# Start of a fused attention and gated-MLP kernel: x's first tile turned ahead of the modulation columns, K's upper half loaded ahead of x's second tile, the first chunk of x taken tile by tile, and units 0 and 1 by pairs of heads

## The chip, the cores and the metric

One core of a Trainium2 chip runs the whole kernel. TensorE (PE) multiplies matrices and turns tiles, VectorE (DVE), ScalarE (ACT) and GpSimd (POOL) do elementwise work, and SyncE's queue (SP) issues nearly all DMAs. Each engine takes its instructions in the order of the program; they meet only through semaphores. The metric is the device time in microseconds (us) of one execution.

## The reference

The inputs are x (2048 x 512), a cache of keys and values (8 groups of 2048 x 128), wq, wo, the MLP's weights, a conditioning vector c and its matrix w_mod, all bf16.

```python
mod = (_silu(c) @ w_mod).reshape(c.shape[0], 6, 1, -1)
sa, ca, ga, sb, cb, gb = ...
h = _layernorm(x, axis=-1) * (1 + ca) + sa
x = x + ga * _A_ref(h, A_k_cache, A_v_cache, A_wq, A_wo)
h = _layernorm(x, axis=-1) * (1 + cb) + sb
x = x + gb * _B_ref(h, B_w_in, B_w_sp, B_b_sp, B_w_out)
```

`_A_ref` is attention with 32 query heads on 8 key/value groups (4 heads to a group): q = h wq, p = softmax(q kT / sqrt(128)), o = p v, then o wo. `_B_ref` is a gated MLP: z = gelu(h w_in), its second half is normalised and mixed over positions by w_sp, multiplied with the first half, then w_out.

## The kernel before

**Units.** The attention is cut into 128 units. Unit u is one group of keys and values and one tile of 128 rows of x (16 tiles, four of them a *chunk* of 512 rows). An iteration `it` of the main loop (from L1455) has 8 slots. In slot i of iteration u, `qk(u, i)` (L1016) computes scores into one of two `s_ps` buffers in PSUM and ACT writes their exp to `pTs[u]`. A unit from 1 on multiplies, for all four heads, two key tiles a slot: two matmuls of 512 columns (L1068), then one exp (L1075). Unit 0 goes by pairs of heads: its slots 0 to 3 do heads 0 and 1 for all sixteen key tiles, slots 4 to 7 heads 2 and 3, with four matmuls of 256 columns a slot (L1052, L1059). `pv(u, i)` (L1116) is one of eight parts of p v (8 matmuls, L1124); parts 0 to 3 are heads 0 and 1, parts 4 to 7 heads 2 and 3; after each four, DVE takes the reciprocal of the row sums and writes `onorm` (L1135, L1136). In the early units, p v of unit u runs in iteration u + 1. Unit 0, going by pairs, starts in its own slots 4 to 7 and ends in slots 0, 2, 4 and 6 of iteration 1.

**What stands around a slot.** `at(it, slot, fn)` runs `fn` ahead of the slot's scores; `fill[it, slot]` runs behind its `pv`. This order of emission is the order of each engine's instructions.

**The start.** SP's queue loads x's tile 0, w_mod's first two parts (`wmod_a`, the columns for sa and ca, in two loads), half of wq's first group (heads 0 and 1), K's lower half by rows in two loads (`k_nat`), then x's tile 1, wq's second half, x's tiles 2 and 3, K's upper half by a DMA transpose (L759), v, the rest of x, and wo. PE multiplies zeros (`warm`, L777) while it waits, then computes the modulation columns (`mod_first`, L874; one matmul of one column for each of 4 x 8 blocks), turns x's tile 0 (L909) between the third and fourth of `mod_first`, and turns K's lower half (`k_turn`, L864), which DVE copies to `kT0`. `modc` (L916) holds 1 + ca and sa; `ln1_mod` (L804) applies them to turned x and writes `hT`. `first_q(0)` (L935) projects q of tile 0 for heads 0 and 1, and `first_q(1)` for heads 2 and 3.

**The first chunk.** x's tiles 1 to 3 are normalised and turned within the first units: `ln_stats` (L695, DVE), `rstd_of` (L675, POOL), `normalise` (L685, DVE), `ln1_turn` (L814: turns on PE, `ln1_mod` on DVE). Tile 1 is done by itself, tiles 2 and 3 together (one `rstd_of`, one turn of both, L1294), and q by `qproj` (L955; matmuls L967, copy on DVE L978): tile 1 in slots 4 and 5 of unit 0, tiles 2 and 3 together in 256 columns in unit 1. The buffers `misc` and `o_ps` in PSUM have two banks each.

**Later chunks.** `ln1_at` (L1302) sets the same for chunks 1 to 3: statistics, norm, four DMA transposes (`ln1_dma`, L833), and the modulation in place (`ln1_dma_mod`, L838). Chunk 1 has its statistics ahead of slot 7 of unit 0, norms ahead of slot 2 of unit 1, DMAs ahead of slot 3, and modulation ahead of slot 2 of unit 2. Its projection for units 4 to 7 (`set_fill`, b = 1, matmuls of 512 columns) starts in slot 5 of unit 2, two matmuls a slot, and needs the modulated chunk.

Of the kernel before, what the change touches and what calls it, by code (L numbers as in the profile page):

```python
# [15 lines left out]
P = 128  # L16
# [559 lines left out]
def kernel(  # L576
# [173 lines left out]
    nc.sync.dma_start(out=wqs[0][:, :, pairs[0]], in_=wq_dram[:, :, pairs[0]])  # L750
    load_k_nat(0)
    load_k_nat(1)
    nc.sync.dma_start(out=x_sb[:, 1, :], in_=x_dram[:, 1, :])
    nc.sync.dma_start(out=wqs[0][:, :, pairs[1]], in_=wq_dram[:, :, pairs[1]])
    nc.sync.dma_start(out=x_sb[:, 2:CT, :], in_=x_dram[:, 2:CT, :])

    kT0 = early.tile([P, SK], BF16, name="kT")
    groups[0] = dict(kT=kT0)
    nc.sync.dma_start_transpose(out=kT0[:, HK:SK], in_=A_k_cache[0, 0, HK:SK])  # L759
    load_v(0)  # L760
    for ch in range(1, NCH):
        tiles = slice(ch * CT, (ch + 1) * CT)
# [48 lines left out]
            op1=ALU.add,  # L811
        )

    def ln1_turn(j0, n, xns, banks=("misc", "o_ps")):  # L814

        ch, c0 = j0 // CT, (j0 % CT) * P
        hT = hT_of(ch)
        for half in range(2):
            t_ps = bank(banks[half])[:].bitcast(BF16).rearrange("p (k q) -> p k q", k=2)
            for k in range(2):  # L820
                dt = half * 2 + k
                for jj in range(n):
                    nc.tensor.transpose(
                        t_ps[:, k, jj * P : (jj + 1) * P],
                        xns[jj][:, dt * P : (dt + 1) * P],
                        ident[:],
                    )
            for k in range(2):
                dt = half * 2 + k
                dst, src = hT[:, dt, c0 : c0 + n * P], t_ps[:, k, 0 : n * P]  # L830
                ln1_mod(dst, src, dt)

    def ln1_dma(j0, n, xns):  # L833
        hT = hT_of(j0 // CT)
# [64 lines left out]
    nc.vector.tensor_copy(out=sc_bf[:], in_=sc[:])  # L899
    xns0 = ln1_norm(0, 1, rstd0)  # L900
    mc_ps = bank("misc")
    warm(11)
    for kt in range(NDT - 1):
        mod_first(kt, mc_ps)
    warm(1)

    x_ps = bank("misc")[:].bitcast(BF16)[:, 0:D]
    for dt in range(NDT):
        nc.tensor.transpose(  # L909
# [1 line left out]
        )  # L911
    xT0 = res.tile([P, D], BF16, name="xn1", bufs=4)
    nc.vector.tensor_copy(out=xT0[:], in_=x_ps)
    warm(2)
    mod_first(NDT - 1, mc_ps)
    nc.vector.tensor_copy(out=modc[:, 0 : 2 * NDT], in_=mc_ps[:, 0 : 2 * NDT])  # L916
    warm(1)
    k_copy = k_turn((0, 1, 2, 3))
    hT_of(0)
    for dt in range(NDT):  # L920
        dst, src = hTs[0][:, dt, 0:P], xT0[:, dt * P : (dt + 1) * P]
# [7 lines left out]
            )  # L929
        else:  # L930
            ln1_mod(dst, src, dt, nc.gpsimd if dt == 3 else nc.vector)
    k_copy()
    qTs = {0: early.tile([P, REP, 512], BF16, name="qT")}

    def first_q(hf):  # L935
# [14 lines left out]
        )  # L950

    first_q(0)
    k_turn((4, 5, 6, 7))()

    def qproj(b, heads, c0, n, banks=("misc", "misc")):  # L955

# [59 lines left out]
    def qk(u, i):  # L1016
        g, j = divmod(u, NT)
        b, jj = g * NCH + j // CT, j % CT
        if i == 0:
            if homes[u] == "wsp":  # L1020
                pTs[u] = wspp.tile([P, NT, 512], BF16, name="wsp")
            else:
                pTs[u] = late.tile([P, NKT, 512], BF16, name=homes[u], bufs=1)
            if by_rows(u):
                rsums[u] = stat.tile([P, NSLOT], FP32, name="rs")
        s_ps = bank2()
        if by_rows(u):
            hh, half = divmod(i, 2)
            for c in range(2):
                k0 = (2 * half + c) * 512  # L1030
                nc.tensor.matmul(  # L1031
                    s_ps[:, c * 512 : (c + 1) * 512],
                    lhsT=qTs[b][:, hh, jj * P : (jj + 1) * P],
                    rhs=groups[g]["kT"][:, k0 : k0 + 512],
                    start=True,
                    stop=True,
                )
            nc.scalar.activation(  # L1038
                out=rows_of(u, hh)[:, half * HK : (half + 1) * HK],
                in_=s_ps[:],  # L1040
                func=ACT.Exp,
                scale=inv_sqrt_dh,
                accum_out=rsums[u][:, i : i + 1],
            )
            if half == 1:
                at(*divmod(u * NSLOT + i + 1, NSLOT), lambda: turn_rows(u, hh))
            return
        if u == 0:
            pair, k0 = i // 4, i % 4 * 4
            qs = slice(pair * 256, (pair + 1) * 256)  # L1050
            for kt in range(4):
                nc.tensor.matmul(  # L1052
                    s_ps[:, kt * 256 : (kt + 1) * 256].rearrange("p (r q) -> p r q", r=2),
                    lhsT=groups[g]["kT"][:, (k0 + kt) * P : (k0 + kt + 1) * P],
                    rhs=qTs[b][:, 2 * pair : 2 * pair + 2, jj * P : (jj + 1) * P],
                    start=(kt % 2 == 0),
                    stop=(kt % 2 == 1),
                )
            nc.scalar.activation(  # L1059
                out=pTs[u][:, k0 : k0 + 4, qs],  # L1060
                in_=s_ps[:].rearrange("p (k q) -> p k q", k=4),
                func=ACT.Exp,
                scale=inv_sqrt_dh,
            )
            return
        for h in range(2):
            kt = 2 * i + h
            nc.tensor.matmul(  # L1068
                s_ps[:, h * 512 : (h + 1) * 512].rearrange("p (r q) -> p r q", r=REP),
                lhsT=groups[g]["kT"][:, kt * P : (kt + 1) * P],  # L1070
                rhs=qTs[b][:, :, jj * P : (jj + 1) * P],
                start=True,
                stop=True,
            )
        nc.scalar.activation(  # L1075
            out=pTs[u][:, 2 * i : 2 * i + 2, :],
            in_=s_ps[:].rearrange("p (k q) -> p k q", k=2),
            func=ACT.Exp,
            scale=inv_sqrt_dh,
        )  # L1080
# [197 lines left out]
    wsp = [None] * NCH  # L1278

    fill = {}  # L1280
    def first_norm():
        first["r1"] = ln1_stats(1, 1)
        ln_stats(mv1, 2, x_sb[:, 2, :])
        first_q(1)
        first["x1"] = ln1_norm(1, 1, first["r1"])

    def first_turn():
        ln1_turn(1, 1, first["x1"])
        ln_stats(mv1, 3, x_sb[:, 3, :])
        first["r2"] = rstd_of(mv1[:, 2:4, :], 2, "ln1")  # L1290

    fill[0, 1] = [first_norm]
    fill[0, 2] = [first_turn]
    at(0, 5, lambda: first.update(x2=ln1_norm(2, 2, first["r2"])))  # L1294
    at(0, 7, lambda: ln1_turn(2, 2, first["x2"], ("misc", "misc")))
    next_q = qproj(0, list(range(REP)), P, P)
    fill[0, 4], fill[0, 5] = next_q[0:8], next_q[8:16]
    rest_q = qproj(0, [0, 1], 2 * P, 2 * P) + qproj(0, [2, 3], 2 * P, 2 * P)
    for i in range(6):
        fill[1, i + 1] = rest_q[(8 * i + 2) // 3 : (8 * i + 10) // 3]  # L1300

    def ln1_at(ch, stats, norm, turn):  # L1302
        st = {}
# [2 lines left out]
        at(norm[0], norm[1] + 1, lambda: ln1_dma(ch * CT, CT, st["x"]))  # L1306
        at(*turn, lambda: ln1_dma_mod(ch))

    ln1_at(1, (0, 7), (1, 2), (2, 2))
    ln1_at(2, (2, 4), (3, 1), (4, 5))  # L1310
    ln1_at(3, (5, 1), (5, 5), (7, 4))
    at(1, 4, lambda: nc.sync.dma_start(out=wmod_b, in_=wmod_dram[:, :, 2 * D : NMOD]))
# [142 lines left out]
    for it in range(NU + 6):  # L1455
        if it < NU:
            if it % CT == 0 and it // CT + 1 < NB:
                set_fill(it // CT + 1)
        elif it == NU:
            free_a.close()  # L1460
            z2p = fast.enter_context(tc.tile_pool(name="z2p", bufs=1))
            zs["z2"] = z2p.tile([P, NT, FH], BF16, name="z2")
        pvs = [u for u in range(max(it - 5, 0), min(it, NU)) if pv_at(u) == it]
        wos = [u for u in range(max(it - 8, 0), min(it, NU)) if wo_at(u) == it]
        wf = [fn for u in wos for fn in wo_proj(u)]
        for i in range(NSLOT):
            for fn in later.pop((it, i), []):
                fn()
            if it < NU:
                qk(it, i)  # L1470
            if it < 2:
                if it == 0 and i >= NSLOT // 2:
                    pv(0, i - NSLOT // 2)
                elif it == 1 and i % 2 == 0:
                    pv(0, (NSLOT + i) // 2)
            elif len(pvs) == 1:
                pv_part(pvs[0], i, NSLOT)
            elif pvs:
# [196 lines left out]
```

## Time and profile before

| What | Value |
|---|---|
| Time, median of 3 runs | 1307.65 us (1307.35 to 1308.0) |
| The profiled execution's own time | 1308.09 us |
| Its span, first to last instruction | 1306.1 us |
| Granted TensorE clock | 0.999 |
| First score matmul | 9.84 us |
| Unit 1, 2, 3, 4: first score matmul | 18.28, 26.60, 35.08, 44.31 us |
| ACT in unit 1 | 8 exps in 7.66 us |
| HBM | 21.37 MB read, 2.10 MB written |

A profile is one execution. Busy time is the sum of an engine's instructions; a line of the timeline gives start and duration in us, the engine, the kernel's line, the operation, output <- inputs, and in brackets the idle time before it and what released it. A matmul's duration holds its way through the array, so pace is read from one start to the next. "SPq" is a DMA being issued by SP's queue, not its transfer. The change lies within the first 45 us.

### The profile page before, as it was taken

To read this page: it belongs to the slowest core of one execution; us is meant where nothing else is said; L and a number is where in the kernel's file an instruction comes from. 1 tells how busy PE (TensorE), PEld (TensorE's weight loads), DVE (VectorE), ACT (ScalarE), POOL (GpSimd) and SP (SyncE) were. 2 spreads that over 40 slices of the span, in tenths; PEclk is the share of its full clock that TensorE was granted. 3 is DMA by queue.
4 is the path that set the end of the run, shared out by engine and by line. 5 is a ranking of instruction groups with operands and counts; after the bars stand their busy time and mean duration, and the time that the engine had idled before them with its cause. 6 is when DMAs were issued, how large, how long until landed. Compare 5 with 4: busy or idle time off the path is not lost.

```text
span 1306.1 us, 22924 instructions
## 1 busy us (share of the span) xinstructions
PE 1297.3 (99%) x8818; PEld 706.9 (54%) x8818; DVE 674.0 (52%) x1740; ACT 1112.4 (85%) x1651; POOL 57.1 (4%) x93
## 2 busy tenths in 40 slices
PE   9999999999999999999999999999999999999998
PEld 6665555555555555555555555555555566644445
DVE  5534445544554455445544554455455557684443
ACT  7899999999999999999999999999999989650000
POOL 1000000000000000000000000000000135210000
PEclk9999999999999999999999999999999999999999
DMA  7569999999999999999999999999999931264300
GB/s 185 123 128 190 161 192 184 190 167 187 192 187 167 192 166 186 188 176 183 186 188 173 185 189 183 179 185 169 187 183 175 158 91 33 55 137 97 79 20 31
DMA packets 743878, 203.33 MB, mean 156 GB/s; under 512 B 728144, under 2 KB 742096, under 8 KB 743760
## 3 DMA queue, kind: packets, MB, share of 16 engines
q1 hardware_dynamic: 741312, 199.68, 83.3%
q10 hardware_dynamic: 2448, 2.10, 0.5%
q8 instruction: 71, 1.16, 0.4%
q14 instruction: 47, 0.39, 0.1%
HBM read 21.37 MB, written 2.10 MB: 18 GB/s over the span
## 4 chain that ended last, share of the span: by engine, by line
PE 92%; DVE 0%; POOL 0%; issue 0%
PE o_ps L1103 20%; PE s_ps L1031 19%; PE o_ps L1124 13%; PE s_ps L1068 12%; PE misc L1181 8%; PE misc L967 7%; PE misc L1542 7%; PE s_ps L1372 2%; PE s_ps L1411 2%; PE o_ps L1575 1%; PE s_ps L1575 0%; POOL xacc L1197 0%; POOL x_sb L1198 0%; PE o_ps L846 0%; DVE bnst L697 0%; DVE tmp L1587 0%
## 5 line engine op out<-in xcount | busy, mean ns | idle before, releaser
L1031 PE MATMUL s_ps<-kT,qT 128*128 128x512 bf16 x1184 | 352.1, 379 | 0.2 <-ACT pn L1038 0.2
L1038 ACT ACTIVATE win_sb<-s_ps 128x1024 bf16<-128x1024 f32 x298 | 304.7, 1023 | 3.2 <-ACT win_sb L1038 0.5
L1103 PE MATMUL o_ps<-pT,v 128*128 128x512 bf16 x896 | 265.8, 379 | 0.0
L1075 ACT ACTIVATE pT<-s_ps 128x1024 bf16<-128x1024 f32 x248 | 250.7, 1025 | 16.3 <-PE s_ps L1068 4.6
L1068 PE MATMUL s_ps<-qT,kT 128*128 128x512 bf16 x848 | 252.2, 379 | 1.1 <-ACT pT L1075 1.1
L1174 DVE SCALAR_TENSOR_TENSOR xacc<-misc,rall,xacc 128x512 f32<-128x512 f32 x290 | 217.0, 748 | 54.6 <-PE misc L1181 48.4
L1038 ACT ACTIVATE pn<-s_ps 128x1024 bf16<-128x1024 f32 x196 | 200.5, 1023 | 1.2
L1181 PE MATMUL misc<-wo_g,oT 128*128 128x512 bf16 x512 | 194.0, 379 | 0.1
L1103 PEld LDWEIGHTS <-v 128*128 128x128 bf16 x1184 | 115.9, 98 | 139.7
L1075 ACT ACTIVATE wsp<-s_ps 128x1024 bf16<-128x1024 f32 x176 | 179.5, 1023 | 13.2 <-PE s_ps L1068 5.0
L967 PE MATMUL misc<-hT,wq_g 128*128 128x512 bf16 (+2 forms) x528 | 190.0, 371 | 0.0
L1031 PEld LDWEIGHTS <-qT 128*128 128x128 bf16 x1184 | 115.5, 98 | 103.9 <-issue 0.7
L1124 PEld LDWEIGHTS <-pT 128*128 128x128 bf16 x2048 | 136.8, 98 | 58.2
L978 DVE CAST qT<-misc 128x512 bf16<-128x512 f32 x127 | 87.2, 687 | 155.5 <-PE misc L967 155.5
L1124 PE MATMUL o_ps<-v,pT 128*128 128x129 bf16 x2048 | 157.2, 220 | 0.0
L1092 DVE TENSOR_TENSOR tot<-rs 128x1 f32<-128x1 f32 x296 | 45.5, 154 | 163.9 <-ACT win_sb L1038 110.2
L1068 PEld LDWEIGHTS <-kT 128*128 128x128 bf16 x848 | 82.2, 98 | 85.7 <-DVE qT L978 1.5
L1124 PEld LDWEIGHTS <-wsp 128*128 128x128 bf16 x1408 | 94.3, 98 | 41.5
L1124 PE MATMUL o_ps<-v,wsp 128*128 128x129 bf16 x1408 | 108.5, 220 | 0.0
L1542 PE MATMUL misc<-wsp,z 128*128 128x512 bf16 (+2 forms) x560 | 100.5, 336 | 0.0
L1038 ACT ACTIVATE wmod_a<-s_ps 128x1024 bf16<-128x1024 f32 x98 | 100.2, 1023 | 0.0
L1103 PE MATMUL o_ps<-wsp,v 128*128 128x512 bf16 x288 | 85.7, 379 | 0.0
(111 smaller groups left out, 874.0 us busy)
## 6 DMA issues: line engine op xcount, KB each, us to landing
wo_g<-in_A_wo_dram SPq DMA_DIRECT2D x8, 512.0 KB, 4.9
wq_g<-in_A_wq_dram SPq DMA_DIRECT2D x7, 512.0 KB, 4.1
v<-in_A_v_cache_dram SPq DMA_DIRECT2D x7, 512.0 KB, 4.9
wsp<-in_w_mod_dram SPq DMA_DIRECT2D x1, 2048.0 KB, 8.6
out_dram<-yout ACTq DMA_DIRECT2D x16, 128.0 KB, 1.7
pT<-win_sb SPq DMA_TRANSPOSE x113, 4.8
win_sb<-in_B_w_in_dram SPq DMA_DIRECT2D x1, 1792.0 KB, 7.3
x_sb<-in_A_x_dram SPq DMA_DIRECT2D x3, 512.0 KB, 5.6
```

The lines of the kernel that those rows point to most:

```text
L967: nc.tensor.matmul(ps[0][:, o0 : o0 + n], lhsT=wqs[g][:, dt, hh * DH : (hh + 1) * DH], rhs=hTs[ch][:, dt, c0 : c0 + n], start=(dt == 0), s ...
L978: nc.vector.tensor_copy(out=dst, in_=src)
L1031: nc.tensor.matmul(s_ps[:, c * 512 : (c + 1) * 512], lhsT=qTs[b][:, hh, jj * P : (jj + 1) * P], rhs=groups[g]["kT"][:, k0 : k0 + 512], sta ...
L1038: nc.scalar.activation(out=rows_of(u, hh)[:, half * HK : (half + 1) * HK], in_=s_ps[:], func=ACT.Exp, scale=inv_sqrt_dh, accum_out=rsums[u ...
L1068: nc.tensor.matmul(s_ps[:, h * 512 : (h + 1) * 512].rearrange("p (r q) -> p r q", r=REP), lhsT=groups[g]["kT"][:, kt * P : (kt + 1) * P], ...
L1075: nc.scalar.activation(out=pTs[u][:, 2 * i : 2 * i + 2, :], in_=s_ps[:].rearrange("p (k q) -> p k q", k=2), func=ACT.Exp, scale=inv_sqrt_dh,)
L1092: nc.vector.tensor_tensor(out=tot[:], in0=rs[:, 2 * hh : 2 * hh + 1], in1=rs[:, 2 * hh + 1 : 2 * hh + 2], op=ALU.add)
L1103: nc.tensor.matmul(o_pss[u][:], lhsT=groups[g]["v1"][:, kt, 0:DH], rhs=pTs[u][:, kt, :], start=(kt == 0), stop=(kt == NKT - 1),)
L1124: nc.tensor.matmul(o_ps[:, hh % 2, 0 : DH + 1], lhsT=pTs[u][:, kt, hh * P : (hh + 1) * P], rhs=groups[g]["v1"][:, kt, 0 : DH + 1], start=( ...
L1174: nc.vector.scalar_tensor_tensor(out=xa[:], in0=X_ps[:], scalar=scale, in1=xa[:], op0=ALU.mult, op1=ALU.add)
L1181: nc.tensor.matmul(ps[0][:], lhsT=oTs[u][:, hh, :], rhs=groups[g]["wo"][:, hh, :], start=(hh == 0 or each), stop=(hh == REP - 1 or each),)
L1542: nc.tensor.matmul(g_pss[f][:, :n], lhsT=z2[:, st, f * P : (f + 1) * P], rhs=wsp[t][:, st, c0 : c0 + n], start=(st == 0), stop=(st == NT - ...
```

## The change

- The order of SP's queue: K's upper half (the DMA transpose) comes ahead of x's tile 1, wq's second half and x's tiles 2 and 3.
- x's tile 0 is turned ahead of all `mod_first`; the `warm` matmuls are 10 and 3 in place of 11, 1, 2 and 1; both `k_turn` follow `first_q(0)`.
- `first_q(1)` moves from behind slot 1 to behind slot 2 of unit 0, ahead of tile 1's norm.
- Tiles 1, 2 and 3 of x are each normalised, turned (four turns into one bank) and projected alone: `tile_stats`, `tile_norm`, `ln1_turn`, `tile_q`. Tile 3's statistics come behind slot 3 of unit 1, its turn behind slot 7, its q in slots 1 and 3 of unit 2.
- Unit 1 goes by pairs of heads, as unit 0. Its p v starts in its own slots 4 to 7 and ends in slots 0, 2, 4 and 6 of iteration 2; unit 0's ends in slots 0 to 3 of iteration 1.
- Chunk 1's statistics come behind slot 7 of unit 0 and slot 0 of unit 1, its `rstd_of` ahead of slot 1, its norms behind slot 2, its DMAs ahead of slot 3 of unit 1, and its modulation ahead of slot 4 of unit 2.

```diff
     load_k_nat(1)
+    kT0 = early.tile([P, SK], BF16, name="kT")
+    groups[0] = dict(kT=kT0)
+    nc.sync.dma_start_transpose(out=kT0[:, HK:SK], in_=A_k_cache[0, 0, HK:SK])
     nc.sync.dma_start(out=x_sb[:, 1, :], in_=x_dram[:, 1, :])
     nc.sync.dma_start(out=wqs[0][:, :, pairs[1]], in_=wq_dram[:, :, pairs[1]])
     nc.sync.dma_start(out=x_sb[:, 2:CT, :], in_=x_dram[:, 2:CT, :])
-    nc.sync.dma_start_transpose(out=kT0[:, HK:SK], in_=A_k_cache[0, 0, HK:SK])
     load_v(0)
...
-    def ln1_turn(j0, n, xns, banks=("misc", "o_ps")):
...
+    def ln1_turn(j, xn):
+
+        ch, c0 = j // CT, (j % CT) * P
         hT = hT_of(ch)
+        t_ps = bank("misc")[:].bitcast(BF16)[:, 0:D]
+        for dt in range(NDT):
+            cols = slice(dt * P, (dt + 1) * P)
+            nc.tensor.transpose(t_ps[:, cols], xn[:, cols], ident[:])
+        for dt in range(NDT):
+            ln1_mod(hT[:, dt, c0 : c0 + P], t_ps[:, dt * P : (dt + 1) * P], dt)
...
-    warm(11)
-    for kt in range(NDT - 1):
-        mod_first(kt, mc_ps)
-    warm(1)
+    warm(10)
     x_ps = bank("misc")[:].bitcast(BF16)[:, 0:D]
...
-    warm(2)
-    mod_first(NDT - 1, mc_ps)
+    for kt in range(NDT):
+        mod_first(kt, mc_ps)
     nc.vector.tensor_copy(out=modc[:, 0 : 2 * NDT], in_=mc_ps[:, 0 : 2 * NDT])
-    warm(1)
-    k_copy = k_turn((0, 1, 2, 3))
+    warm(3)
...
-    k_copy()
...
     first_q(0)
-    k_turn((4, 5, 6, 7))()
+    for kts in ((0, 1, 2, 3), (4, 5, 6, 7)):
+        k_turn(kts)()
...
-        if u == 0:
+        if u < 2:
             pair, k0 = i // 4, i % 4 * 4
...
+    def tile_stats(j):
+        first[j] = ln1_stats(j, 1)
+
+    def tile_norm(j):
+        xn = res.tile([P, D], BF16, name="xn2", bufs=2)
+        normalise(xn[:], x_sb[:, j, :], mv1[:, j, 0:1], first[j][:, 0:1])
+        first[j] = xn
+
+    def tile_q(j):
+        return qproj(0, list(range(REP)), j * P, P)
+
+    def chunk_stats(j0):
+        for j in range(j0, j0 + 2):
+            ln_stats(mv1, j, x_sb[:, j, :])
+
+    fill[0, 1] = [lambda: tile_stats(1)]
+    fill[0, 2] = [lambda: first_q(1), lambda: tile_norm(1)]
+    fill[0, 3] = [lambda: ln1_turn(1, first[1]), lambda: tile_stats(2)]
+    at(0, 5, lambda: tile_norm(2))
+    q1, q2, q3 = tile_q(1), tile_q(2), tile_q(3)
+    fill[0, 5], fill[0, 6] = q1[0:8], q1[8:16] + [lambda: ln1_turn(2, first[2])]
+    fill[0, 7] = [lambda: chunk_stats(CT)]
+    fill[1, 0] = [lambda: chunk_stats(CT + 2)]
+    at(1, 1, lambda: first.update(r=rstd_of(mv1[:, CT : 2 * CT, :], CT, "ln1")))
+    fill[1, 1] = q2[0:8]
+    fill[1, 2] = q2[8:16] + [lambda: first.update(x=ln1_norm(CT, CT, first["r"]))]
+    at(1, 3, lambda: ln1_dma(CT, CT, first["x"]))
+    fill[1, 3] = [lambda: tile_stats(3)]
+    fill[1, 5] = [lambda: tile_norm(3)]
+    fill[1, 7] = [lambda: ln1_turn(3, first[3])]
+    fill[2, 1], fill[2, 3] = q3[0:8], q3[8:16]
+    at(2, 4, lambda: ln1_dma_mod(1))
...
-    ln1_at(1, (0, 7), (1, 2), (2, 2))
     ln1_at(2, (2, 4), (3, 1), (4, 5))
...
-            if it < 2:
-                if it == 0 and i >= NSLOT // 2:
-                    pv(0, i - NSLOT // 2)
-                elif it == 1 and i % 2 == 0:
-                    pv(0, (NSLOT + i) // 2)
+            if it < 2 and i >= NSLOT // 2:
+                pv(it, i - NSLOT // 2)
+            elif it == 1:
+                pv(0, i + NSLOT // 2)
+            elif it == 2 and i % 2 == 0:
+                pv(1, (NSLOT + i) // 2)
+            elif it < 3:
+                pass
             elif len(pvs) == 1:
```

More of the change, by code (lines that the diff above doesn't have):

```diff
@@ L755 @@
     nc.sync.dma_start(out=x_sb[:, 2:CT, :], in_=x_dram[:, 2:CT, :])
-    kT0 = early.tile([P, SK], BF16, name="kT")
-    groups[0] = dict(kT=kT0)
-    nc.sync.dma_start_transpose(out=kT0[:, HK:SK], in_=A_k_cache[0, 0, HK:SK])
     load_v(0)
@@ L812, in ln1_mod @@
         )
-    def ln1_turn(j0, n, xns, banks=("misc", "o_ps")):
-        ch, c0 = j0 // CT, (j0 % CT) * P
+    def ln1_turn(j, xn):
+        ch, c0 = j // CT, (j % CT) * P
         hT = hT_of(ch)
[L818 to L831, printed above, removed]
+        t_ps = bank("misc")[:].bitcast(BF16)[:, 0:D]
[4 more added lines that the diff above has]
+            ln1_mod(hT[:, dt, c0 : c0 + P], t_ps[:, dt * P : (dt + 1) * P], dt)
     def ln1_dma(j0, n, xns):
@@ L1280 @@
     fill = {}
[L1281 to L1300, printed above, removed]
+    def tile_stats(j):
[26 more added lines that the diff above has]
+    at(2, 4, lambda: ln1_dma_mod(1))
     def ln1_at(ch, stats, norm, turn):
```

## The prediction

> **What bounds the kernel now.** I read the page first (busy time, slices, the chain that ended last), then busy time by stage, the waits, and the timelines of the first 62 us, the only stretch that the change touches.
>
> ```profile
> span 1306.1 us, 22924 instructions
> PE 1297.3 (99%) x8818; PEld 706.9 (54%) x8818; DVE 674.0 (52%) x1740; ACT 1112.4 (85%) x1651; POOL 57.1 (4%) x93
> ...
> PE 92%; DVE 0%; POOL 0%; issue 0%
> ```
>
> TensorE (PE) bounds the kernel as a whole. So the change pays only through PE time without useful work ahead of the point where PE runs unbroken, and costs only through new PE waits. Busy time by stage, cut at the first score matmul and at the starts of units 1, 2, 3 and 4:
>
> ```profile
> core 0: us, PE busy (x) PEld busy (x) DVE busy (x) ACT busy (x) POOL busy (x), PEclk, DMA share, GB/s
> 0.00:9.84 9.84, 8.28 (x68) 4.14 (x69) 4.05 (x16) 2.35 (x4) 2.31 (x12) 1.00 0.87 253
> 9.84:18.28 8.44, 7.81 (x101) 6.93 (x100) 6.53 (x19) 7.00 (x8) 1.75 (x4) 1.00 1.16 302
> 18.28:26.60 8.32, 7.26 (x67) 4.84 (x65) 7.08 (x20) 8.26 (x9) 1.28 (x2) 1.00 0.19 45
> 26.60:35.08 8.48, 8.48 (x87) 5.87 (x88) 3.76 (x11) 7.32 (x9) 0.00 (x0) 1.00 0.66 193
> 35.08:44.31 9.23, 9.23 (x91) 6.16 (x90) 6.04 (x16) 7.47 (x9) 1.27 (x2) 1.00 0.74 166
> ```
>
> Unit 0 is limited now by PE, now by ACT; unit 1 by ACT (8.26 of 8.32), with PE idle about 1.1; from unit 2 on PE has no gap. In unit 1 VectorE (DVE) is at 7.08 of 8.32: hardly slack. The rows that matter below:
>
> ```profile
> 5.89 2.25 SPq L759 DMA_TRANSPOSE kT<-in_A_k_cache_dram  x1
> 8.14 0.17 DVE L916 COPY modc<-misc 128x8 f32<-128x8 f32 x1 [0.19 <-PE misc L874]
> 9.84 1.03 PE L1052 MATMUL s_ps<-qT,kT 128*128 128x256 bf16 x8 [0.24 <-ACT qT L947]
> 23.42 1.38 DVE L686 TENSOR_SCALAR xn<-x_sb,mv,rstd_ln 128x512 bf16<-128x512 bf16 x4 [0.97 <-POOL rstd_ln L682]
> 23.87 6.01 SPq L836 DMA_TRANSPOSE hT<-xn  x4
> 26.60 0.60 PE L1068 MATMUL s_ps<-qT,kT 128*128 128x512 bf16 x2 [1.06 <-ACT pT L1075]
> 31.21 1.38 DVE L805 TENSOR_SCALAR hT<-hT,modc 128x512 bf16<-128x512 bf16 x4 [4.67 <-DMA hT<-xn]
> 32.01 0.59 PE L967 MATMUL misc<-hT,wq_g 128*128 128x512 bf16 x2
> 35.08 0.59 PE L1068 MATMUL s_ps<-qT,kT 128*128 128x512 bf16 x2
> ```
>
> First scores start at 9.84. Unit 2 starts late, at 26.60, where PE had waited for q (copied 25.86 to 26.54). The second chunk of x is normalised at 23.42, turned by four DMAs from 23.87, usable from 31.6 (first modulated slice), and first used at 32.01: 0.4 to spare.
>
> **Paces** (start to start in these timelines): a slot's scores on PE 0.435 (4 of 256 columns or 2 of 512); a PV part 0.455; 8 projections of 128 columns 0.44; 4 turns 0.23; one exp on ACT 0.945, released 0.64 after its scores start (0.71 in the 512 form), freeing its bank 0.14 after its pace. DVE: statistics of a tile 0.80, normalising 0.32 (0.13 more until a reader starts), reciprocal with onorm 0.54, q copy 0.585, modulating a 128-column slice from PSUM 0.26. POOL: 0.17 after the statistics, then 0.31 and 0.58 (one tile) or 1.05 (four), 0.06 to the reader. Followed engine by engine in program order, these paces put the kernel before at 26.54, 35.13 and 37.77 for the starts of unit 2, unit 3 and slot 2 of unit 3; the trace has 26.60, 35.08 and 37.71.
>
> **The start.** K's DMA transpose now takes the place in SP's queue of x's second tile (3.70), and no longer waits for the modulation load (0.7 of SP wait). It holds SP for 2.25, so x's second tile is issued at 5.95 instead of 3.70, wq's second half at 6.4 and x's tiles 2-3 at 6.9. The loads behind (v, the rest of x, wo) come about 0.8 earlier than now, as the 0.7 is gone. On PE, x's tile 0 is normalised at 5.54, so its four turns run at 5.60 to 6.03 (0.107 each, half the pace of the filler matmuls' 0.43). The 33 modulation matmuls need 0.69 + 0.22 (as at 5.92 and 7.76): 6.94. The last modulation slice was issued at 1.6 and took 4.9: it is there at 6.5. Now modc came 0.18 after its last matmul, first_q 0.57 after modc's start: 7.69. Fillers fall from 15 to 13 and lie in the shadow of modc. K's turns follow first_q by 0.51 (as 8.71 to 9.22), their copy starts 0.42 later and lasts 0.42, with 0.05 to the reader: first scores at 9.1, 0.74 earlier. Both ends: 8.7 if the turns run at full pace, 10.15 by the third rival.
>
> **Slots 0 to 3.** Slot 2 waits for the first exp: 9.1 + 0.64 + 1.08 = 10.81. first_q(1), now behind it, runs at 11.25, its DVE copy at 11.95, and behind that copy on DVE the norm of tile 1 at 12.28; its turn on PE waits 0.5 until 12.73. Slot 4 comes at 12.96 (now 13.38). q and turns by tile cost PE nothing: 32 matmuls of 0.055 for 16 of 0.1085; DVE pays 12 slices of 0.26 for what were 4 of 0.26 and 4 of 0.32, 0.8 more.
>
> **Slot 4 to the end of unit 1.** PE is full: 0.89 a slot, 0.44 more in four of them (q of tiles 1 and 2), 0.23 for tile 2's turn: 12.96 + 12 x 0.89 + 4 x 0.44 + 0.23, about 25.65 at the end of unit 1's last PV part. There the new order puts tile 3's turn, and DVE is not there. DVE's queue: tile 2's slices end 18.33; reciprocal and onorm 18.87; the four statistics of the next chunk 22.07; POOL's rstd of it 23.66; four norms 24.94; reciprocal and onorm 25.48; only then tile 3's statistics 26.28; POOL 27.40; norm 27.85. **PE waits 2.2**, and behind the waiting turn stands unit 2's first score, so ACT starves too (its last exp of unit 1 ends near 26.2, the next starts at 28.8). Now tiles 2 and 3 share one rstd and are turned at 16.94, long before. Unit 2 starts at 28.08 against 26.60.
>
> **Units 2 and 3.** Unit 2 has four PV parts less (moved into unit 1) and tile 3's 16 projections more: 0.94 less for PE, so ACT's pace sets it: 28.08 + 7.75 = 35.83, against 8.48 now. The next chunk's turned x is no new wait: its norms start at 23.66 (now 23.42), DMAs and modulation keep 7.8, but the q copy of tile 3 is ahead on DVE: first slice from 32.47, usable 32.9, first needed 33.1. Then DVE is late once more: modulation to 33.76, statistics to 36.96, reciprocal and onorm 37.50, and only then the copy of b=1's head 0 (38.17), whose bank head 2 wants at 38.05: 0.12. Slot 2 of unit 3: 38.60.
>
> **Sum**, after against before: lead at unit 1's start 17.64 - 18.28 = -0.64; unit 1 10.44 - 8.32 = +2.12; unit 2 7.75 - 8.48 = -0.73; first two slots of unit 3 +0.14: +0.89, less the 0.06 by which the paces overshoot: +0.83. Behind it order and work are the same. The profiled execution took 1308.09 (span 1306.1 and 2.0 around it), so 1308.9 for it; against the median of 1307.65: **1308.5**. That is 0.06%, and about 0.2% (2.6 us) is what a measurement of this kernel can tell from no change: no change, on the slow side.
>
> **Rivals.**
>
> *The turn of tile 3 finds its data* (DVE is quicker than its rows, or the wait is absorbed). Against it: four statistics, five norms and two round trips to POOL in one in-order queue. What is late next caps it: q of tile 3 needs slices that are no sooner; and b=1's first projection cannot start before the turned chunk, 31.45 + 0.4 = 31.85 against 32.01, so -0.2: 1307.5. Only if that chain shortens too does ACT's pace rule: unit 3 at 25.9 + 7.6 = 33.5, 1.6 earlier: 1306.0. Even then 0.2% is not reached without a start near 8.1.
>
> *Slower: x's second tile is late.* It is queued behind K's transpose. Until 10.36 its landing is hidden by first_q(1)'s copy; from there each us is a us for turn(1), slot 4 and all DVE work behind. Loads of x landed 2.2 to 8.0 after issue in the first 40 us, so between 8.15 and 13.95: price 0 to 3.6. From 12.2 on the total passes 2.6: 1310.3 and more, at 13.95 1312.1. For it: the DMA engines are full (share 1.09 to 1.33) until 18. Against it: the bytes ahead are 1.6 MB and K's 0.26 MB, and the queue moved 2.3 MB by 9.5. I take 9.6, nearest to K's landing (3.70 + 5.3 = 9.0) and 0.13 MB more. The Trainium skill (DMA: Bandwidth & Descriptors, Queues, rings and completion order) has each DMA engine consume descriptors in ring order; by that rule x follows K's packets and the landing is this 9.4 to 9.6, which no run here has shown yet.
>
> *PE's fast pace comes later.* Fillers run at 0.43 until 5.9, a single one at 6.61 still takes 0.59 (0.38 later), and two at 7.33 show 0.21: the pace doubled near 7. The granted clock reads 1.00 throughout. The new order gives PE one filler less before that and four turns instead. If it doubles some 3 us later (the fillers ran 5.8 at half pace), three fillers end at 8.2, first_q at 9.05, K's copy at 10.1: first scores 10.15, +1.05 on everything: 1309.6. The Trainium skill (TensorE: Matmul & The Clock Gate, Part 1 and Part 4) holds that busy windows of about 3.4 us lift the gate and that transposes do not count as busy in the same way, which speaks against this change; by that rule this rival's time would be the forecast. The trace agrees with a doubling after some 5.8 us of activity and shows nothing of the turns' part in it.
>
> **How the numbers follow.** Forecast 56% (1308.0 to 1309.2 with a start between 8.7 and 9.4). Tile 3 in time 12%, of it 5 beyond 0.2%. x late 20%, 18 of them beyond 12.2. Late fast pace 12%, 4 beyond, where x is late as well. So faster 5%, same 73%, slower 22%. Range 1306.2 to 1311.2: from near the first rival's lower time to a landing of x at 13.1; about 2 in 10 are left out.
>
> **What would show it.** Right: a PE wait of about 2.2 for DVE's xn ahead of tile 3's turn, with ACT idle then; first scores near 9.1; unit 2 shorter than before. Wrong: unit 2 starting before 26.6; no such wait; statistics of tile 1 beginning after 10.4; first scores after 9.8; a wait of b=1's first projection for the turned chunk.

## The result, and the profile after

| | before | after |
|---|---|---|
| Time, median of 22 runs each on one chip | 1307.59 us (1307.28 to 1308.02) | 1309.39 us (1308.95 to 1310.84) |
| The profiled execution's time, its span | 1308.09, 1306.1 us | 1309.50, 1307.0 us |
| First score matmul | 9.84 us | 9.06 us |
| Units 1, 2, 3, 4 | 18.28, 26.60, 35.08, 44.31 us | 17.64, 28.02, 35.63, 45.16 us |

The ratio of after to before is 1.0017, with a 95% interval of 1.0011 to 1.0023: slower, by less than the 0.2% that the text on record took as what can be told from no change, though the interval lies off 1. The 22 times of after are in two groups, 12 from 1308.95 to 1309.50 and 10 from 1310.33 to 1310.84, with nothing between. Those of before lie within 0.75 us. The profile of after is one of the lower group.

First the page of after: its first lines, and the chain that ended last by engine.

```profile
span 1307.0 us, 22836 instructions
PE 1288.1 (99%) x8691; PEld 708.4 (54%) x8848; DVE 674.6 (52%) x1744; ACT 1112.7 (85%) x1651; POOL 57.9 (4%) x95
...
PE 91%; issue 1%; DVE 0%; POOL 0%
```

PE still bounds the whole, so only PE's gaps ahead of the even part count. Here is after's busy time by stage, cut at the first score matmul and at the starts of units 1 to 4 (length, then each engine's busy time, the granted clock, DMA):

```profile
0.00:9.06 9.06, 7.34 (x65) 3.77 (x66) 4.00 (x16) 2.35 (x4) 2.32 (x12) 1.00 0.85 246
9.06:17.64 8.58, 7.53 (x97) 6.71 (x98) 5.17 (x15) 7.01 (x8) 1.60 (x4) 1.00 1.17 309
17.64:28.02 10.38, 8.38 (x120) 7.85 (x117) 8.20 (x25) 8.29 (x9) 2.07 (x4) 1.00 0.26 66
28.02:35.63 7.61, 7.56 (x72) 4.95 (x71) 5.08 (x15) 6.75 (x8) 0.00 (x0) 1.00 0.77 211
35.63:45.16 9.53, 9.35 (x91) 6.21 (x90) 6.21 (x16) 7.84 (x9) 1.28 (x2) 1.00 0.58 161
```

The third row is the one to read: unit 1 grew from 8.32 to 10.38, and PE is busy for 8.38 of it. The 2 us without work are one wait, the longest in after's waits of PE (6 to 50 us):

```profile
PE misc L820 <- DVE xn L686: 2.4, 2, 2.0
```

The timelines show where it lies. First PE's of after (start, duration, engine, line, operation):

```profile
25.17 0.62 PE L1110 MATMUL o_ps<-v,pT 128*128 128x129 bf16 x8
27.79 0.40 PE L820 MATMUL misc<-ident,xn 128*128 128x128 bf16 x4 [2.00 <-DVE xn L686]
28.02 0.59 PE L1054 MATMUL s_ps<-qT,kT 128*128 128x512 bf16 x2
```

DVE's of after, in the same stretch:

```profile
22.01 0.66 DVE L964 CAST qT<-misc 128x512 bf16<-128x512 f32 x1
23.59 1.38 DVE L686 TENSOR_SCALAR xn<-x_sb,mv,rstd_ln 128x512 bf16<-128x512 bf16 x4 [0.91 <-POOL rstd_ln L682]
24.88 0.16 DVE L1121 RECIPROCAL rall<-o_ps 128x2 f32<-128x2 f32 x1
25.08 0.42 DVE L1122 TENSOR_TENSOR onorm<-o_ps,rall 128x256 bf16<-128x256 f32 x1
25.42 0.68 DVE L697 BATCH_NORM_STATS2 bnst<-x_sb 128x6 f32<-128x512 bf16 x1
...
27.32 0.41 DVE L686 TENSOR_SCALAR xn<-x_sb,mv,rstd_ln 128x512 bf16<-128x512 bf16 x1 [1.00 <-POOL rstd_ln L682]
```

And ACT's of after, the first exps of unit 2:

```profile
28.72 2.85 ACT L1061 ACTIVATE pT<-s_ps 128x1024 bf16<-128x1024 f32 x3 [2.21 <-PE s_ps L1054]
```

PE's last p v part of unit 1 starts at 25.17. Next in PE's order is the turn of x's tile 3, whose norm DVE does at 27.32. DVE itself first stood 0.91 for POOL's result for the next chunk, then did that chunk's four norms (23.59) and p v's reciprocal and product, and only at 25.42 the statistics of tile 3, which cost another round to POOL (1.00). DVE is busy for 8.20 of 10.38 in this stage: it is late not by its load but by its order. ACT has no scores meanwhile and stands 2.21.

### The profile page after: what moved, and what is told of

It reads as the page before. It is cut to its first block, busy times and chain, and to the rows that moved or that the text cites. A ratio compares the mean times of both kernels' runs of the same rounds, so it can differ in the third digit from the quotient of the medians.

```text
span 1307.0 us, 22836 instructions
## 1 busy us (share of the span) xinstructions
PE 1288.1 (99%) x8691; PEld 708.4 (54%) x8848; DVE 674.6 (52%) x1744; ACT 1112.7 (85%) x1651; POOL 57.9 (4%) x95
## 4 chain that ended last, share of the span: by engine, by line
PE 91%; issue 1%; DVE 0%; POOL 0%
PE s_ps L1017 19%; PE o_ps L1089 19%; PE o_ps L1110 13%; PE s_ps L1054 12%; PE misc L1167 8%; PE misc L1542 7%; PE misc L953 7%; PE s_ps L1369 2%; PE s_ps L1408 2%; PE o_ps L1575 1%; PE s_ps L1575 0%; POOL xacc L1183 0%; POOL x_sb L1184 0%; PE o_ps L837 0%; DVE bnst L697 0%
## 5 line engine op out<-in xcount | busy, mean ns | idle before, releaser
L1017 PE MATMUL s_ps<-kT,qT 128*128 128x512 bf16 x1160 | 346.9, 379 | 2.5 <-ACT pn L1024 0.2
L1089 PE MATMUL o_ps<-pT,v 128*128 128x512 bf16 x862 | 258.5, 379 | 1.1
L1061 ACT ACTIVATE pT<-s_ps 128x1024 bf16<-128x1024 f32 x240 | 243.1, 1026 | 17.2 <-PE s_ps L1054 5.8
L1054 PE MATMUL s_ps<-qT,kT 128*128 128x512 bf16 x832 | 247.4, 379 | 1.2
L1167 PE MATMUL misc<-wo_g,oT 128*128 128x512 bf16 x478 | 181.2, 379 | 1.1 <-DVE xacc L1160 0.3
L953 PE MATMUL misc<-hT,wq_g 128*128 128x512 bf16 (+1 forms) x506 | 175.8, 364 | 0.7
```

The source lines that it names most:

```text
L953: nc.tensor.matmul(ps[0][:, o0 : o0 + n], lhsT=wqs[g][:, dt, hh * DH : (hh + 1) * DH], rhs=hTs[ch][:, dt, c0 : c0 + n], start=(dt == 0), s ...
L1017: nc.tensor.matmul(s_ps[:, c * 512 : (c + 1) * 512], lhsT=qTs[b][:, hh, jj * P : (jj + 1) * P], rhs=groups[g]["kT"][:, k0 : k0 + 512], sta ...
L1054: nc.tensor.matmul(s_ps[:, h * 512 : (h + 1) * 512].rearrange("p (r q) -> p r q", r=REP), lhsT=groups[g]["kT"][:, kt * P : (kt + 1) * P], ...
L1061: nc.scalar.activation(out=pTs[u][:, 2 * i : 2 * i + 2, :], in_=s_ps[:].rearrange("p (k q) -> p k q", k=2), func=ACT.Exp, scale=inv_sqrt_dh,)
L1089: nc.tensor.matmul(o_pss[u][:], lhsT=groups[g]["v1"][:, kt, 0:DH], rhs=pTs[u][:, kt, :], start=(kt == 0), stop=(kt == NKT - 1),)
L1167: nc.tensor.matmul(ps[0][:], lhsT=oTs[u][:, hh, :], rhs=groups[g]["wo"][:, hh, :], start=(hh == 0 or each), stop=(hh == REP - 1 or each),)
```

## The experiments

The runs were made in three sets, each on a chip of its own, with runs of the kernel before beside it (medians 1307.76 of 33, 1307.73 of 27 and 1307.85 of 33 on the three chips). The questions in order: which half of the change costs; whether the price of tile 3's wait is what the prediction made it; and what makes the upper group.

### The halves

The start alone, on the kernel before: K's transpose and PE's new order, but x's tiles, units 0 and 1 as before.

```diff
     load_k_nat(1)
+    kT0 = early.tile([P, SK], BF16, name="kT")
...
-    warm(11)
...
+    warm(10)
...
+    for kt in range(NDT):
+        mod_first(kt, mc_ps)
```

> The start alone: K's upper half loaded ahead of x's second tile, x's first tile turned ahead of the modulation columns, 10 and 3 fillers, both turns of K behind first_q(0); the units as before. Theory A (the start is a gain of some 0.7 that the units give back; the two levels of the changed kernel's times, near 1309.1 and near 1310.7, come from the start, through PE's pace doubling later): first scores near 9.06; units 1, 2 and 3 at 18.0, 26.3 and 34.9; time 0.3 below the kernel before in its lower level, and a second level about 1.5 above it in a part of the executions. Theory B (the levels come from the units, or from the chip): one level, 0.3 below the kernel before.

Measured: 1308.23 us, ratio 1.0004 (0.9995 to 1.0013), in one group but for 1308.86 and 1309.89. Both theories had it 0.3 below the kernel before; it came 0.5 above the median of 1307.76 on its chip. A copy of the kernel before ran beside it:

> The kernel before once more, for the spans of its executions: theory A: one level, 1307.3 to 1308.0, with spans of about 1305.5 to 1306.1. If the two levels were the chip's, they show here as well.

It gave 1307.91 (ratio 1.0002, 0.9993 to 1.0011). Its first scores came at 9.59 and its unit 2 at 26.35, so the start of before moves by a quarter of a us from one execution to the next (the units alone, below, have the same start and 9.95), and the profile on which the prediction rested was a late one: its span is 1306.1, the copy's 1305.7. Against this copy the start alone led by 0.28 at the first scores (9.31), and was 0.62 behind at unit 2 (26.97). Where it lost it, in the start alone's timeline of DVE:

```profile
11.48 0.69 DVE L697 BATCH_NORM_STATS2 bnst<-x_sb 128x6 f32<-128x512 bf16 x1 [0.74 <-DMA x_sb<-in_A_x_dram]
```

and in its timeline of PE:

```profile
13.07 0.28 PE L822 MATMUL misc<-ident,xn 128*128 128x128 bf16 x2 [1.33 <-DVE xn L686]
```

Before's order has the statistics of x's tile 2 on DVE ahead of tile 1's norm. With x's loads behind K's transpose, tile 2 is not there until 11.48, and tile 1's turn on PE waits 1.33 for what stands behind it on DVE. So late loads of x do cost, as one of the rivals said, though here it is tile 2, where the rival had tile 1. They cost nothing in the changed kernel, where tile 2's statistics come later (the first half of the change needs the second). The two groups of times do not come from the start.

The other half alone: the old start, with tiles and units as in the change.

```diff
-        if u == 0:
+        if u < 2:
...
+    fill[0, 1] = [lambda: tile_stats(1)]
...
+            if it < 2 and i >= NSLOT // 2:
+                pv(it, i - NSLOT // 2)
```

> The units alone: the first chunk tile by tile, units 0 and 1 by pairs of heads, the start as before. Theory A: PE waits 2.2 for DVE's norm of tile 3 at the end of unit 1; units 2 and 3 at 28.8 and 36.6, unit 4 at 46.0; 1.6 slower than the kernel before, in one level. Theory B (the units make the levels): two levels some 1.5 apart. If the loss came from the order of the loads and not from DVE's queue, this one is as fast as the kernel before.

Measured: 1310.25 us, ratio 1.0022 (1.0013 to 1.0031); six times from 1309.61 to 1310.25, four from 1311.18 to 1311.34, and one of 1313.22. The wait of 2.00 ahead of tile 3's turn is there (28.67), and so are the two groups, as theory B had it.

### The wait itself

Tile 3's statistics and norm ahead of the next chunk's statistics:

```diff
-    fill[0, 7] = [lambda: chunk_stats(CT)]
-    fill[1, 0] = [lambda: chunk_stats(CT + 2)]
+    fill[0, 7] = [lambda: tile_stats(3), lambda: chunk_stats(CT)]
+    fill[1, 0] = [lambda: tile_norm(3), lambda: chunk_stats(CT + 2)]
...
-    fill[1, 3] = [lambda: tile_stats(3)]
-    fill[1, 5] = [lambda: tile_norm(3)]
```

> The changed kernel with tile 3's statistics ahead of the next chunk's (behind slot 7 of unit 0) and its norm behind slot 0 of unit 1; its turn stays behind slot 7 of unit 1. Theory A (what is late next takes the place of the wait): the 2.0 wait ahead of tile 3's turn is gone and unit 2 starts at 25.9 instead of 28.0; then q of tile 3 waits 0.9 for DVE's slices and the first projection of the next chunk 1.2 for its turned x, so that unit 3 starts at 35.6 as in the changed kernel, and the time is that of the changed kernel within 0.3. Rival (the wait itself is the loss): 1.5 to 2.0 faster than the changed kernel, at or below the kernel before.

Measured: 1308.37 us, ratio 1.0006 (0.9997 to 1.0015). The turn ran at 25.83 without a wait, and unit 2 began at 26.06. Then the waits went where the text put them, but smaller: 0.38 of the next chunk's first projection for the turned chunk (32.34), and unit 4 at 44.65. The chunk's DMAs were issued at 25.36 and used at 31.87, 6.5 later, where the prediction carried on with before's 7.8 from the norms (7.3 from the issue). So a miss in size: the wait was worth more than the text let it be.

This version with two more moves, to take the waits that it still had: the turn two slots earlier, and the next chunk's projections two slots later.

```diff
-    fill[1, 7] = [lambda: ln1_turn(3, first[3])]
+    fill[1, 5] = [lambda: ln1_turn(3, first[3])]
...
-                it, slot = 2 + (10 + k) // 16, (5 + k // 2) % 8
+                it, slot = 2 + (14 + k) // 16, (7 + k // 2) % 8
```

> The changed kernel with three moves: tile 3's statistics ahead of the next chunk's and its norm behind slot 0 of unit 1; its turn behind slot 5 of unit 1 instead of slot 7; the projections of the next chunk from slot 7 of unit 2 instead of slot 5. Theory A (what was late next was the turned chunk): no wait for tile 3, none for the chunk; units 3 and 4 at 33.5 and 43.7 against 35.6 and 45.2 in the changed kernel and 35.1 and 44.3 before; 0.8 faster than the kernel before, in one level. Rival (DVE's extra slices or ACT bind in unit 2): no faster than the kernel before.

Measured: 1307.27 us, all 11 within 1306.96 to 1307.47, ratio 0.9996 (0.9987 to 1.0005), 0.5 below before's median on its chip where 0.8 was expected. Unit 4 came at 43.64. No wait of PE behind 13 us is longer than 0.3.

The smallest edit came last: tile 3's statistics alone, two slots earlier, into the 0.91 in which DVE stood for POOL.

```diff
-    fill[1, 2] = q2[8:16] + [lambda: first.update(x=ln1_norm(CT, CT, first["r"]))]
+    fill[1, 2] = q2[8:16] + [lambda: tile_stats(3), lambda: first.update(x=ln1_norm(CT, CT, first["r"]))]
...
-    fill[1, 3] = [lambda: tile_stats(3)]
```

> The changed kernel with the statistics of x's tile 3 moved ahead of the next chunk's norms (two slots earlier; the norm and the turn of tile 3 stay where they are). On DVE they fill the 0.9 us in which it waits for POOL, so the norm of tile 3 comes at about 25.4 instead of 27.32 and the PE wait at the turn falls from 2.0 to 0.1 or 0.2; unit 2 starts near 26.05. Some of the gain is given back at the turned chunk (its first projection waits, as in e3_tile3_early): about 0.8 below the changed kernel's lower level, so 1308.4. The clock theory: no PE gap of more than 0.4 us in units 1 and 2, so the upper level (about +1.3) is gone but for the one in ten that other kernels show: 0 to 2 of 11. The rival (the two levels come with unit 1 by pairs of heads, whatever the gap): half or so of the executions stay 1.3 above the others.

Measured: 1307.27 us, ten within 1307.02 to 1307.79 and one of 1308.44; ratio 0.9997 (0.9988 to 1.0006). Its timeline of DVE:

```profile
22.72 0.69 DVE L697 BATCH_NORM_STATS2 bnst<-x_sb 128x6 f32<-128x512 bf16 x1
23.44 0.18 DVE L698 BATCH_NORM_AGGREGATE mv<-bnst 128x2 f32<-128x6 f32 x1
23.71 1.38 DVE L686 TENSOR_SCALAR xn<-x_sb,mv,rstd_ln 128x512 bf16<-128x512 bf16 x4
...
25.55 0.41 DVE L686 TENSOR_SCALAR xn<-x_sb,mv,rstd_ln 128x512 bf16<-128x512 bf16 x1
...
30.67 1.38 DVE L804 TENSOR_SCALAR hT<-hT,modc 128x512 bf16<-128x512 bf16 x4
```

and its timeline of PE:

```profile
25.30 0.62 PE L1110 MATMUL o_ps<-v,pT 128*128 128x129 bf16 x8
26.01 0.40 PE L820 MATMUL misc<-ident,xn 128*128 128x128 bf16 x4
26.25 0.59 PE L1054 MATMUL s_ps<-qT,kT 128*128 128x512 bf16 x2
...
31.20 0.64 PE L953 MATMUL misc<-hT,wq_g 128*128 128x512 bf16 x2
```

The statistics fill DVE's own wait: the four norms start at 23.71 against 23.59, tile 3's norm at 25.55 against 27.32, and the turn has no wait written beside it. The expected loss at the turned chunk did not come: DMAs issued from 24.16 were usable by 30.67, and the first projection ran at 31.20 unhindered. Unit 4 started at 43.45, 1.71 ahead of after. As expected the upper group is gone. The gain against the changed kernel's lower group, expected at 0.8, was 2.0 (1307.27 against 1309.27, the middle of the three lower times of the changed kernel on the same chip), and 3.4 against its median there.

### The two groups

A second run of the changed kernel, on another chip, caught the upper group in its profile.

> The changed kernel once more, beside the others. All theories: two levels, near 1309.1 and near 1310.7, each in about half of the executions, and a lead of 1.5 to 3 for the kernel before.

Measured: 1310.67 us, ratio 1.0021 (1.0012 to 1.0030), 9 of 11 in the upper group. Its timeline of PE:

```profile
27.62 0.40 PE L820 MATMUL misc<-ident,xn 128*128 128x128 bf16 x4 [2.01 <-DVE xn L686]
27.86 0.59 PE L1054 MATMUL s_ps<-qT,kT 128*128 128x512 bf16 x2
28.29 0.69 PE L1110 MATMUL o_ps<-v,pT 128*128 128x129 bf16 x8
28.78 1.06 PE L1054 MATMUL s_ps<-qT,kT 128*128 128x512 bf16 x2
29.63 1.06 PE L953 MATMUL misc<-hT,wq_g 128*128 128x128 bf16 x8
30.48 1.06 PE L1054 MATMUL s_ps<-qT,kT 128*128 128x512 bf16 x2
31.34 0.99 PE L1110 MATMUL o_ps<-v,pT 128*128 128x129 bf16 x8
32.16 0.59 PE L1054 MATMUL s_ps<-qT,kT 128*128 128x512 bf16 x2
```

And its windows of 1 us (length, the engines' busy times, then the granted clock, DMA share, GB/s):

```profile
28.00:29.00 1.00, 1.00 (x12) 0.73 (x10) 1.00 (x5) 0.45 (x1) 0.00 (x0) 0.85 0.69 80
29.00:30.00 1.00, 1.00 (x6) 0.52 (x5) 0.16 (x1) 0.70 (x2) 0.00 (x0) 0.50 0.68 131
30.00:31.00 1.00, 1.00 (x9) 0.72 (x7) 0.00 (x0) 0.89 (x1) 0.00 (x0) 0.50 0.65 127
31.00:32.00 1.00, 1.00 (x9) 0.72 (x8) 0.00 (x0) 0.42 (x1) 0.00 (x0) 0.50 0.51 57
32.00:33.00 1.00, 1.00 (x14) 0.76 (x13) 0.00 (x0) 0.81 (x2) 0.00 (x0) 0.95 0.70 164
```

The wait is the same 2.01 as in the lower group. But about 1 us after it the same two score matmuls take 1.06 in place of 0.59, and the next starts 0.85 later in place of 0.43 or 0.44: the granted clock is 0.50 from about 28.7 to 32.1. In the lower group's profile it reads 1.00 in each of these windows. A busy PE does not show this; pace and clock do. Some 3.4 us at half pace would lose 1.7. From tile 3's turn (27.62 against 27.79) to unit 4 (46.62 against 45.16) this execution loses 1.63 against the first profile; the groups lie about 1.4 apart.

If the stand-still of PE is the cause, work in it should help, and a longer one should do worse. Nine matmuls of zeros ahead of the turn, twice, with the changed kernel again beside the second:

```diff
-    fill[1, 7] = [lambda: ln1_turn(3, first[3])]
+    fill[1, 7] = [lambda: warm(9), lambda: ln1_turn(3, first[3])]
```

> The changed kernel with nine matmuls on zeros (1.9 at full pace) ahead of tile 3's turn, inside its 2.2 wait, so that PE does not stand still there. Theory C (the second level is PE's clock: the 2 us in which PE stands still at the end of unit 1 make it fall back to half pace in some executions): the lower level stays near 1309.1 and the upper one, near 1310.7, is gone. Theory D (the levels come from something else in the units, such as when a DMA lands): two levels as in the changed kernel, unchanged by fillers.

> The kernel of e6_fillers once more (nine zero matmuls ahead of tile 3's turn, no PE gap there), for more executions: 3 of 11 were in the upper level. Clock theory: the share stays well below that of the changed kernel on the same chip; at most 3 of 11, lower level 1309.0 to 1309.6. If fillers do nothing for the clock: as many as in e12_after_again.

> The changed kernel once more, as the mate of the three others on this chip: lower level 1309.0 to 1309.5, upper level 1310.3 to 1311.0, and 4 to 9 of 11 in the upper one (19 of 33 so far).

Measured: with fillers 1309.53 (ratio 1.0015, 1.0006 to 1.0024), 3 of 11 in the upper group, and 1309.18 (ratio 1.0011, 1.0002 to 1.0020), 1 of 11. The changed kernel on the second of these chips had 1310.67 (ratio 1.0020, 1.0011 to 1.0029), 8 of 11 in the upper one. So 4 of 22 with fillers against 17 of 22 without, on the same two chips. The lower group did not move, as the turn still starts when DVE is done (27.70 and 27.83). The timeline of PE of the second run with fillers:

```profile
25.66 2.11 PE L776 MATMUL o_ps<-onorm 128*128 128x512 bf16 x9
27.83 0.40 PE L820 MATMUL misc<-ident,xn 128*128 128x128 bf16 x4
28.06 0.59 PE L1054 MATMUL s_ps<-qT,kT 128*128 128x512 bf16 x2
```

Tile 3's statistics four times, three of them to no use, for a longer stand-still:

```diff
-    fill[1, 3] = [lambda: tile_stats(3)]
+    fill[1, 3] = [lambda: [ln_stats(mv1, 3, x_sb[:, 3, :]) for _ in range(3)], lambda: tile_stats(3)]
```

> The changed kernel with tile 3's statistics taken four times over: DVE reaches its norm 2.4 later, so the wait of PE ahead of tile 3's turn grows from 2.2 to 4.6, and all behind it comes 2.4 later (unit 4 at 47.7 instead of 45.3). Theory C: PE falls back in most or all executions and the profile shows half pace behind the wait (8 PV matmuls in about 0.9 instead of 0.45) for up to 3.4; time 3.5 to 4.5 above the lower level of the changed kernel, with few executions at 2.4. Theory D: 2.4 above each of the two levels of the changed kernel, in the same proportion, at full pace.

Measured: 1315.53 us in 5 runs (1314.71 to 1315.97), ratio 1.0058 (1.0044 to 1.0072), all in one group, some 6.2 above the changed kernel's lower one. The wait was 4.39; its windows of 1 us:

```profile
27.00:28.00 1.00, 0.00 (x0) 0.00 (x0) 0.95 (x4) 0.00 (x0) 0.00 (x0) 1.00 0.33 65
28.00:29.00 1.00, 0.00 (x0) 0.00 (x0) 0.75 (x2) 0.00 (x0) 0.13 (x1) 0.72 0.63 127
29.00:30.00 1.00, 0.00 (x0) 0.00 (x0) 0.22 (x1) 0.00 (x0) 0.66 (x2) 0.50 0.67 139
...
35.00:36.00 1.00, 1.00 (x12) 0.77 (x11) 0.00 (x0) 0.82 (x1) 0.00 (x0) 0.86 0.98 401
```

The clock fell at about 28.4, while PE stood, and came back at about 35.3: half pace for 5 us of work (30.25 to 35.3), which costs 2.5, beside the 2.4 of the longer wait. DVE's last operation ends 4.87 later than in the first profile of the changed kernel (1307.65 against 1302.78), as these two would have it. The rest of the 6.2 lies behind that operation: 6.0 from there to the end of the span, against 4.2 (what lies around the span was 1.9, against 2.5). So of the 2 by which the expectation was too low, half pace for 5 us in place of 3.4 accounts for 0.8; why the end is longer is open.

And a shorter one, of about 1 us: the smallest edit above with one more statistics of tile 2 ahead of tile 3's norm.

```diff
-    fill[1, 2] = q2[8:16] + [lambda: first.update(x=ln1_norm(CT, CT, first["r"]))]
+    fill[1, 2] = q2[8:16] + [lambda: tile_stats(3), lambda: first.update(x=ln1_norm(CT, CT, first["r"]))]
...
-    fill[1, 3] = [lambda: tile_stats(3)]
+    fill[1, 3] = [lambda: ln_stats(mv1, 2, x_sb[:, 2, :])]
```

> As e9_no_wait, with one more statistics of 0.8 us (of tile 2, written again with the same values) on DVE ahead of tile 3's norm, so the PE wait at the turn is about 1.0 us. Unit 2 near 26.9; lower level 1308.4 to 1308.8. If the clock falls only after a gap near 2 us: 0 to 2 of 11 in the upper level. If the share of executions goes with the length of the gap (4.4 us: all, 2.0 us: 19 of 33): about 3 of 11. The rival (not the gap): half of the executions.

Measured: 1308.08 us, ten within 1307.70 to 1308.39 and one of 1309.28; ratio 1.0003 (0.9994 to 1.0012). The wait was 0.90. So a stand-still of 0.9 us put 1 of 11 executions at most in an upper group, one of 2.0 us 27 of 44 (three samples of the changed kernel), and one of 4.4 us 5 of 5. From 11 executions this 1 cannot be told from the 3 that a share in step with the length would give. Unit 2 at 26.68 and the time of 1308.08 are a little better than expected, for the reason seen in the smallest edit.

## Why the prediction was right, and where it was not

**Right, with sizes.** Tile 3's turn waits for DVE: 2.2 forecast, 2.16 measured in the prediction's own way (from 25.17 and a part's pace of 0.455 to 27.79; the 2.00 of the trace counts from the end of the last matmul). The stations of the prediction's sum against after's trace: slot 4 of unit 0 at 12.96 and 12.90, the turn at 27.85 and 27.79, unit 2 at 28.08 and 28.02, unit 3 at 35.83 and 35.63, slot 2 of unit 3 at 38.60 and 38.56. First scores were put at 9.1 and came at 9.06. The span grew by 0.9, the sum's +0.83. The smallest edit shows that it is this wait: without it the kernel is 2.0 below the changed kernel's lower group.

**What was luck.** The measured 1309.39 lies in the stated range, 0.2 above the forecast's own band (1308.0 to 1309.2). That it is so near is the luck of 12 lower executions in 22: in the two later samples the same kernel has 1310.67, still in the range, but 2.2 above the forecast of 1308.5. As the text called anything within 0.2% no change, that answer could not tell a right sum from one that had left out the clock.

**x's second tile.** The landing was taken as 9.6. DVE began tile 1's statistics at 9.37 in the first profile of the changed kernel; in the ten other profiles with this order of loads it waited 0.18 to 0.29 for the DMA and began between 9.30 and 9.82. All lie ahead of the 10.36 from which the landing costs, so this rival did not come. K's transpose held SP's queue for 1.72 to 2.19, where the sum had 2.25. By the ring order that the Trainium skill (DMA: Bandwidth & Descriptors, Queues, rings and completion order) states, the prediction's estimate was 9.4 to 9.6; the traces have 9.30 to 9.82, on both sides of it.

**The fast pace at the start.** It did not come later: the projections for q start at 7.71 with 8 of them in 0.45 (to 8.16), the fast pace, after fillers up to 7.5. Each trace records when the granted clock changes: full clock begins at 6.72 in this profile, at 3.96 to 6.57 in the ten others with the new start, and at 3.99 to 7.22 in the three with the old one (7.22 in the profile on which the prediction rested). So the moment moves by some 3 us from one execution to the next with either order, and the 1.00 that the view gives for the time ahead of it is no reading. The rival was wrong there, and so is the inference from the Trainium skill's rule on transposes (TensorE: Matmul & The Clock Gate, Part 4) for this case: four turns among the fillers cost no time that the traces show. They took only 0.43, so this is no test of the rule itself.

**The step that failed: full pace behind the wait.** The sum took 28.08 + 7.75 for unit 2, and "behind it order and work are the same". By their times that holds in 17 of 44 executions of the changed kernel. In the others, going by the one that was profiled, PE works at half clock for some 3.4 us after the stand-still, which adds about 1.4 and makes the median of two of its three samples 1310.67. The clock was thought of, but at the start of the kernel, not behind the gap that the same text had found. The Trainium skill (TensorE: Matmul & The Clock Gate, Part 1) has the clock fall after at least one idle window of about 3.4 us and stay until a busy one has passed. The lengths agree: 3.41 us at 0.50 after the wait of 2.0 (28.69 to 32.10), and twice that, 6.83 (28.45 to 35.28), around the one of 4.4. The threshold does not: 2.0 us without a matmul was enough in 27 of 44 executions, and a wholly idle window of 3.4 us cannot lie in them. By the advice of the Trainium skill (TensorE: Matmul & The Clock Gate, Why this matters for your kernels), no PE gaps above about 3 us, this gap would have been harmless; the measurement decides.

**The lower group is 0.7 above the forecast too.** 1308.9 was the forecast for the profiled execution, which took 1309.50. The span accounts for 0.1 of it; what lies around the span was 2.5 in place of 2.0. In the second and third samples of the changed kernel it was 2.15 to 2.67, in the copy of before 1.98 to 2.09. Why is open. The rest of the distance between the lower group and 1308.5 goes with before's late profile: the copy started unit 1 at 18.02 in place of 18.28, so 0.26 of the lead of 0.64 forecast there was that execution's own.

**The cap in the first rival.** With tile 3 in time it set the next limit at the turned chunk (31.85, a gain of 0.2 at most, 1307.5), unless the chain shortens as well (1306.0). The smallest edit measured 1307.27 against 1307.85 on its chip, in between: the chunk was usable at 30.67, so that limit was not one. The term that was too long is the DMAs' way: 7.3 us from the issue in before, where DVE did wait for them, and 6.5 or less here.

**A small one.** The first two slots of unit 3, with the late copy on DVE: +0.14 forecast, +0.30 measured (2.93 against 2.63; the whole unit 9.53 against 9.23).

What stays open beside the 0.4 around the span: 4 of 22 executions with fillers are in the upper group, and most of the other kernels have an execution or two some 1 to 1.8 above the rest. None of these was caught in a profile. For the best version, 1307.27 twice (ratios 0.9996 and 0.9997), both intervals reach past 1: 0.5 us ahead of before on its chip is not shown to be faster.

## What to carry to other kernels

When a new PE wait is found, price it twice: the wait itself, and the pace behind it, since a stand-still of some 2 us can halve the clock for 3.4 us more. On an in-order engine look for its own waits (here 0.91 for POOL) and put the late instruction there: one moved line gave back 2.0 us of the lower group's time and took the upper group away. A kernel whose times fall into two groups should be profiled until each group has a profile, for the median alone tells of neither.

## What had not been expected of the hardware

The granted clock fell to 0.50 behind a wait far shorter than the 3.4 us for which it then stayed there. Going by the times, it fell after 0.9 us without PE work in none that is clearly told (1 of 11 at most), after 2.0 us in 27 of 44 executions with the same wait, and after 4.4 us in 5 of 5. Half pace came about 1 us after PE had gone back to work (28.7, where the turn had started at 27.62), not in the gap itself, when the gap was 2.0 us; at 4.4 us it came within the gap.

The fourteen traces' records of the clock say more. Within a trace all changes of the clock lie whole multiples of 3.41 us apart, as 28.69 and 32.10, or 28.45 and 35.28 above. Cut each trace into windows along these marks. From full clock it fell behind every window in which PE had 2.01 us or more without a matmul (2.01 from 25.28 to 28.69 in the second sample of the changed kernel, 2.58 from 25.03 to 28.45 with the long stand-still, 2.17 and more at the kernels' ends), and behind none with 1.98 or less; as the ends of matmuls are modelled, this limit is rough. In the two profiles of the changed kernel's lower group a mark cuts the wait in two, into 1.41 and 0.59 and into 1.04 and 0.96. So where the marks happen to lie seems to decide into which group an execution falls. This fits the profiles and was not tried by a run of its own. It does not fit all: if the marks lie anywhere alike, a limit of 2.0 would catch the wait of 2.0 in 41% of the executions (an estimate, (3.41 - 2.00) / 3.41), and 27 of 44 is more; and it does not explain the 4 of 22 with fillers.
